# The fourth tile's queries and keys made in the first layer's time, and the second batch's means and keys taken in turns with the last values

## The chip, the cores and the metric

The kernel runs on one core of one Trainium2 chip. The time is device microseconds of one execution, and the figure that is compared is the median of several runs. A core has five engines that run side by side and wait for one another through semaphores: PE multiplies matrices, DVE and ACT do element-wise work and read the accumulators that PE writes, POOL does element-wise work in SBUF, and SP issues most of the transfers. Each engine takes its instructions strictly in the order in which they were written, so an instruction that waits holds up all that stand behind it on its engine.

## What is computed

```python
# q, k, v: [2, 8, 768, 64]
k_sum = k.reshape(B, H, 24, 32, D).max(axis=3)       # one key for each block of 32
v_sum = v.reshape(B, H, 24, 32, D).mean(axis=3)      # one value for each block of 32
scores_l = scale * q @ k.T                           # kept where |i - j| < 16, else -1e9
scores_s = scale * q @ k_sum.T + log(32)
a = softmax([scores_l, scores_s])
attn = a @ [v, v_sum]                                # -> x: [1536, 512]
h = x @ w_in                                         # layer one: [1536, 2048]
g = h * clip(h + 3, 0, 6) / 6
x2 = g @ w_out                                       # [1536, 512]
# then: 8 experts of 192 rows each, chosen greedily from the logits x2 @ w_gate,
# out[rows of e] = relu(x2[rows of e] @ w1[e]) @ w2[e]
```

All of it is in float32; a large product is taken as three products of a high and a low part.

## The kernel before, in words

The 1536 rows are cut into 12 tiles of 128 (numbered 0 to 11 in the code; six to a batch), and three tiles make a unit, so that units 0 and 1 are batch 0 and units 2 and 3 are batch 1. A tile `n` goes through attention in two halves of four heads, `(n, 0)` and `(n, 1)`:

- `q_prep(n)` transposes the tile's queries on PE (L343) and copies them with ACT (L345) into `qT`; `window(n)` copies the keys that the tile may see, and the block keys, into `kw` on DVE (L358 to L365).
- `front(n, h)` is the scores on PE (L377), mask and row maximum on DVE (L385, L387). Its argument `after` says whether it also makes the next tile's `q_prep` and `window`.
- `soften()` is the four exponentials on ACT (L397), the reciprocal on DVE (L399, L400) and the scaling on POOL (L401).
- `turn(n, h)` transposes the weights on PE (L409) and copies them with ACT (L414); `values(n, h)` multiplies them with the values on PE (L427). `emit_x()` then makes the tile's high part `xh` with ACT (L449) and its low part `xl` with DVE (L79, named after the line of the scheduler that issues deferred work).
- The values' tile `VW` holds the window's rows, loaded from DRAM, and below them the block means. `vsum_mean` makes the means of a batch on PE (L201), and `vsum_place` copies them into a `VW` with one ACT (L208) and one DVE instruction (L209). In the trace each of the two waits for the other: both read one accumulator.
- `kprep(b)` transposes the keys of batch `b` on PE (L325), copies them with ACT (L328), and takes the block maxima on DVE (L329).

The first layer is `gemm1(u)`: 16 slices `f` of 128 columns, each 12 matmuls (L620, L621, L622: high by high, high by low, low by high) into one accumulator, then a relu on ACT (L623) and the gate on DVE (L637). Its weights arrive as 64-bit words: `w_conv` makes float32 of them with three DVE instructions a slice (L275), `w_split` makes the high part on ACT (L292) and the low part on POOL (L293).

The order on each engine is the order in which the program writes the work, and `drive` sets it: it holds several generators ("streams"), each with a total cost and a span from `lo` to `hi`, and always takes the next step of the stream that is furthest behind, `lo + (hi - lo) * done / total`. Only the steps' yielded costs count, not times. First comes the prologue with the whole attention of unit 0 (`first_unit`). Then the first 8 slices of unit 0 are written in turns with the attention of tiles 3 to 5 and with the preparation of batch 1, then the first 8 slices of unit 1 with the start of tile 6, and so on, until attention is done within unit 2. The second product, the routing and the experts follow and do not take part in the change.

At the end of batch 0 `halves()` first drains what is left of tiles 4 and 5 (`drain`: a `turn`, its `values`, and `emit_x`, one after another), then makes three means, all keys and the other three means of batch 1. Then tile 6 begins: `vsum_place` twice, `q_prep(6)`, `window(6)`.

One point of the order matters more than it shows: `attend_unit(0)` ends when tile 2 is in `finished`, and this happens inside a step, so the step runs on to its next yield. Before, that takes in `front(3, 0)`.

Of the kernel before, what the change touches and what calls it, by code (L numbers as in the profile page):

```python
# [15 lines left out]
B, H, S, D = 2, 8, 768, 64  # L16
# [10 lines left out]
UT = 3  # L27
# [20 lines left out]
MEANS = {(1, 0): range(2), (1, 1): range(2, 4), (2, 0): range(4, 6)}  # L48
LOADS = {(3, 0): [("kraw", 0, j) for j in range(3)], (3, 1): [("kraw", 0, j) for j in range(3, 6)],
         (4, 0): [("vraw", 1, j) for j in range(3)], (4, 1): [("vraw", 1, j) for j in range(3, 5)]}  # L50
ATTS = [29066, 32816, 25780, 17002]
FILL = 6500, 8500
END = [0.92, 0.92, 0.92]
S0 = 0.78
# [35 lines left out]
def build(ctx, tc, q, k, v, w_in, w_out, w_gate, w1, w2, out):  # L90
# [30 lines left out]
    def bank(i):  # L121
        return psum.tile([128, 512], FT, name=f"bank{i}")
# [51 lines left out]
    def v_of(n):  # L174

        return VL if n == UT - 1 else VW[n % 2]
# [17 lines left out]
    def vsum_mean(b, js):  # L194

        for j in js:
            if j == 0:
                mp[b] = bank(5 if b == 0 else 4)
            x = raw.pop(("vraw", b, j))
            at = ZO - WIN - 4 * j  # L200
            PE.matmul(mp[b][:KEYS], zones[:, at:at + KEYS], x.rearrange("p h d -> p (h d)"),  # L201
                      start=j == 0, stop=j == S // 128 - 1)
            if b and j == 0:
                soon.append(partial(load_rows, "vraw", v, b, S // 128 - 1))
# [130 lines left out]
    def q_prep(n, hps=range(HP)):  # L335
        b, i = divmod(n, 6)
        x = raw["qraw", b, i]
        p = bank(6 if n == UT else (7 if n % 2 else 4) if n < UT else (4 if n % 2 else 7))
        a, z = hps[0], hps[-1] + 1
        if a == 0:  # L340
            fr[n] = att.tile([128, HP, 128], FT, name="qT"), att.tile([128, HP, 2, KEYS], FT, name="kw")
        for hp in hps:
            PE.transpose(p[:, hp * 128:(hp + 1) * 128],  # L343
                         x[:, 2 * hp:2 * hp + 2, :].rearrange("p h d -> p (h d)"), ident)
        ACT.activation(fr[n][0][:, a:z], p[:, a * 128:z * 128].rearrange("p (h s) -> p h s", s=128), AF.Copy)  # L345
        if n >= UT and (n + 1) % 6:
            soon.append(partial(load_rows, "qraw", q, *divmod(n + 1, 6)))
# [19 lines left out]
    def front(n, h, after):  # L367
        b, i = divmod(n, 6)
        qT, kw = fr[n]
        A = Abuf[(2 * n + h) % (LAG + 1)]  # L370
        sp = [bank(0), bank(1)]
        for pr in range(2):
            hp = 2 * h + pr
            for g in range(2):
                for s in range(2):
                    r, c = slice(64 * s, 64 * s + 64), slice(QG * g, QG * g + QG)
                    PE.matmul(sp[s][c, pr * KEYS:(pr + 1) * KEYS], qT[r, hp, c], kw[r, hp, g], start=True, stop=True)  # L377
        if after:
            q_prep(n + 1)
        mk = mask[:, 0 if i == 0 else 2 if i == 5 else 1]  # L380
        sm = att.tile([128, 4, 4], FT, name="sm", bufs=2)
        for pr in range(2):
            for s in range(2):
                c = 2 * pr + s
                DVE.tensor_tensor_reduce(out=A[:, c], in0=sp[s][:, pr * KEYS:(pr + 1) * KEYS], in1=mk, scale=1.0,  # L385
                                         scalar=-3e38, op0=OP.add, op1=OP.max, accum_out=sm[:, 0, c:c + 1])
        DVE.tensor_scalar(sm[:, 1], sm[:, 0], -SCALE, None, op0=OP.mult)  # L387
        if after:
            window(n + 1)
        later.append((A, sm))  # L390
# [78 lines left out]
    def first_unit():  # L469

        for n in range(UT):
            for h in range(2):
                if len(pend) >= LAG:
                    t = pend.pop(0)
                    turn(*t)
                    turned.append(t)
                    yield 660
                front(n, h, h == 1)
                pend.append((n, h))
                yield 1250 + 450 * h  # L480
                yield from soften()
                if (n, h) in MEANS:
                    vsum_mean(0, MEANS[n, h])
                    yield 900 * len(MEANS[n, h])
        for n in range(UT):
            vsum_place(0, v_of(n))
            t = pend.pop(0)
            turn(*t)
            turned.append(t)
            yield 660  # L490
            for h in range(2):
                values(*turned.pop(0))
                yield 1000
            yield from emit_x()

    def halves():
        yield from first_unit()
        for n in range(UT, NT):
            b, i = divmod(n, 6)
            if b and i == 0:  # L500
                for x in VW:
                    vsum_place(b, x)
                q_prep(n)
                window(n)
                yield 2400
            for h in range(2):
                t = pend.pop(0) if len(pend) >= LAG else None
                if t:
                    turn(*t)
                    turned.append(t)  # L510
                    yield 660
                after = h == 1 and i < 5
                front(n, h, after)
                pend.append((n, h))
                yield 1250 + 450 * after
                if len(turned) > 1:
                    values(*turned.pop(0))
                    yield 1000
                    yield from emit_x()
                yield from soften()  # L520
                if b + 1 < B:
                    for kind, src, j in LOADS.get((i, h), ()):
                        load_rows(kind, (k, v)[src], b + 1, j)
                if h == 1 and i == 4 and b + 1 < B:
                    load_rows("qraw", q, b + 1, 0)
            if i == 5:
                yield from drain()
                if b + 1 < B:
                    vsum_mean(b + 1, range(3))
                    yield 2700  # L530
                    yield from kprep(b + 1)
                    vsum_mean(b + 1, range(3, S // 128))
                    yield 2700
                    prepared.append(b + 1)

    turned, prepared = [], []
    attention = halves()
# [279 lines left out]
    for u, fs, att_stream, slices in ((0, half[0], [attend_batch(), ATTS[1]], 6),  # L817
                                      (1, half[0], [attend_for(FILL[0]), FILL[0]], 4),
                                      (0, half[1], [attend_for(FILL[1]), FILL[1]], 3),
                                      (1, half[1], [attend_unit(2), ATTS[2] - sum(FILL)], 0)):  # L820
        st = [att_stream + [0.01, 0.95]]
        if slices:
            n = 4 * slices + CLAG * (slices == 3)
            st.append([part(splitting, n), n, 0.0, 0.85 if slices > 3 else S1])
        drive([[gemm1(u, fs), G1 / 2, 0, 1]] + st, soon)
# [436 lines left out]
```

## Time and profile before

| | |
|---|---|
| median of 3 runs | 606.79 us (606.27 to 610.18) |
| the profiled execution | 610.91 us, of which the span from first to last instruction is 609.1 us |
| PE busy | 558.2 us (92% of the span) |
| DVE, ACT, POOL busy | 393.8, 292.3, 162.5 us |
| mean clock granted to TensorE | 0.97 of full speed |

The times of the rows below are microseconds from the start of the span of that execution. The prologue ends and the first layer's products begin at about 47 us; attention lasts until about 215 us. A granted clock of 0.50 is the lower of TensorE's two levels (1.2 GHz), 1.00 the upper (2.4 GHz).

### The profile page before, as it was taken

What the parts mean: (1) busy time and instruction counts of PE and PEld (TensorE: products, weight loads), DVE (VectorE), ACT (ScalarE), POOL (GpSimd) and SP (SyncE); (2) the same over time, 40 slices, a digit from 0 to 9 for tenths busy, and PEclk for the clock granted to TensorE, in tenths of its full rate; (3) what the DMA queues carried; (4) which work ended last, traced back from release to release, by engine and by line L of the source; (5) the groups of instructions that cost most, each with busy time, mean ns of one, the idle gap of its engine ahead of it and who ended that gap; (6) DMA issues with size and microseconds to landing.
All of it is one profiled execution on the core that took longest, in us unless ns stands there. A gap on an engine that the chain in (4) does not pass through costs nothing.

```text
span 609.1 us, 10859 instructions
## 1 busy us (share of the span) xinstructions
PE 558.2 (92%) x3791; PEld 466.4 (77%) x3791; DVE 393.8 (65%) x1204; ACT 292.3 (48%) x699; POOL 162.5 (27%) x194
## 2 busy tenths in 40 slices
PE   7766878899999998889999999999899999999994
PEld 6454756898889987775687777778688889988883
DVE  6546765874543279990007787873568888888880
ACT  4543734654545345451123232233466776776760
POOL 1312421433111024353245444446201001110111
PEclk9956999999999999999999999999899999999998
DMA  9958953311111055420015000003568889988811
GB/s 193 227 144 213 208 133 90 93 48 44 45 28 25 1 174 171 141 70 27 1 39 169 1 1 1 1 2 119 191 179 250 247 262 278 281 234 256 250 63 31
DMA packets 114432, 75.06 MB, mean 123 GB/s; under 512 B 59904, under 2 KB 100864, under 8 KB 114368
## 3 DMA queue, kind: packets, MB, share of 16 engines
q1 hardware_dynamic: 112384, 67.96, 41.6%
q0 software_dynamic: 1984, 6.32, 2.8%
q8 instruction: 32, 0.52, 0.4%
q14 instruction: 32, 0.26, 0.1%
HBM read 67.55 MB, written 6.71 MB: 122 GB/s over the span
## 4 chain that ended last, share of the span: by engine, by line
PE 49%; issue 26%; DVE 8%; POOL 5%; ACT 4%; SPq 4%; DMA 2%; POOLq 0%; DVEq 0%; ACTq 0%
PE bank L620 7%; PE bank L621 7%; PE bank L622 7%; PE bank L740 5%; PE bank L742 5%; PE bank L741 5%; POOL out_dram L1065 2%; PE bank L427 2%; PE bank L933 2%; POOL xs L671 2%; PE bank L649 2%; SPq L171 1%; PE bank L583 1%; PE bank L377 1%; ACT A L397 1%
## 5 line engine op out<-in xcount | busy, mean ns | idle before, releaser
L620 PE MATMUL bank<-x,wh 128*128 128x384 f32 x256 | 92.6, 362 | 1.0 <-DVE t L637 0.9
L302 DVE TENSOR_TENSOR wl<-t,wh 128x1024 fp32r<-128x1024 f32 x64 | 77.1, 1221 | 20.7 <-ACT wh L301 19.1
L717 ACT ACTIVATE work<-t 128x384 fp32r<-128x384 f32 (+2 forms) x80 | 36.3, 459 | 112.2 <-PE bank L741 106.6
L621 PE MATMUL bank<-x,wh 128*128 128x384 f32 x256 | 86.8, 339 | 2.7 <-DVE x L79 2.7
L622 PE MATMUL bank<-x,wl 128*128 128x384 f32 x256 | 87.2, 341 | 1.2 <-POOL wl L293 1.1
L718 POOL TENSOR_TENSOR tlx<-t,work 128x384 fp32r<-128x384 f32 (+1 forms) x58 | 60.6, 1045 | 81.4 <-ACT work L717 78.3
L740 PE MATMUL bank<-wh,work 128*128 128x512 f32 x192 | 78.7, 410 | 1.6 <-ACT work L717 0.8
L623 ACT ACTIVATE t<-bank,three 128x384 f32<-128x384 f32 x64 | 37.1, 580 | 82.4 <-PE bank L622 82.4
L742 PE MATMUL bank<-wh,tlx 128*128 128x512 f32 x192 | 75.8, 395 | 0.1
L741 PE MATMUL bank<-wl,work 128*128 128x512 f32 x192 | 75.6, 394 | 0.0
L1090 PE MATMUL bank<-x,wh 128*128 128x384 f32 x256 | 73.7, 360 | 0.5 <-DVE x L1016 0.5
L301 ACT ACTIVATE wh<-t 128x1024 fp32r<-128x1024 f32 x64 | 65.7, 1048 | 0.0
L637 DVE SCALAR_TENSOR_TENSOR t<-t,bank 128x384 f32<-128x384 f32 x64 | 35.0, 550 | 45.7 <-ACT t L623 45.5
L1092 PE MATMUL bank<-x,wl 128*128 128x192 f32 x256 | 64.2, 251 | 0.0
L1065 POOL DMA_INDIRECT out_dram<-t,idx x16 | 14.9, 934 | 141.6 <-DVE t L1114 136.0
L620 PEld LDWEIGHTS bank<-x,wh 128*128 128x128 f32 x256 | 48.9, 191 | 4.1 <-DVE t L637 1.5
L621 PEld LDWEIGHTS bank<-x,wh 128*128 128x128 f32 x256 | 48.9, 191 | 3.6 <-DVE x L79 3.4
L401 POOL TENSOR_TENSOR A<-A,sm 128x480 f32<-128x480 f32 x24 | 24.3, 1011 | 98.9 <-ACT at L414 47.0
L622 PEld LDWEIGHTS bank<-x,wl 128*128 128x128 f32 x256 | 48.6, 190 | 2.2 <-POOL wl L293 2.2
L1092 PEld LDWEIGHTS bank<-x,wl 128*128 128x128 f32 x256 | 48.9, 191 | 0.3
L1106 PE MATMUL bank<-wh,t 128*128 128x512 f32 x128 | 49.0, 392 | 0.0
L1090 PEld LDWEIGHTS bank<-x,wh 128*128 128x128 f32 x256 | 48.1, 188 | 1.2 <-DVE x L1016 0.8
(188 smaller groups left out, 1082.9 us busy)
## 6 DMA issues: line engine op xcount, KB each, us to landing
t<-in_moe_w_dram SPq DMA_DIRECT2D x128, 256.0 KB
t<-in_moe_w_in_dram SPq DMA_DIRECT2D x16, 512.0 KB
big<-in_moe_w_out_dram SPq DMA_DIRECT2D x16, 512.0 KB
VW<-in_v_dram SPq DMA_DIRECT2D x18, 192.0 KB
t<-in_v_dram SPq DMA_DIRECT2D x12, 256.0 KB
t<-xs SPq DMA_DIRECT2D x8, 258.0 KB
raw<-in_q_dram SPq DMA_DIRECT2D x8, 256.0 KB
t<-in_k_dram SPq DMA_DIRECT2D x12, 128.0 KB
```

The costliest lines, as they stand in the source:

```text
L301: ACT.activation(hi, x, AF.Copy)
L302: DVE.tensor_tensor(lo, x, hi.bitcast(FT), op=OP.subtract)
L620: PE.matmul(p, wh[:, kk, :], xh[:, kk, :], start=kk == 0, stop=False)
L621: PE.matmul(p, wh[:, kk, :], xl[:, kk, :], start=False, stop=False)
L622: PE.matmul(p, wl[:, kk, :], xh[:, kk, :], start=False, stop=kk == KD - 1)
L718: (DVE if placed[0] else POOL).tensor_tensor(ths[i][1], t, ths[i][0].bitcast(FT), op=OP.subtract)
L740: PE.matmul(acc[j], th[:, c], WH[s], start=f == 0, stop=False)
L741: PE.matmul(acc[j], th[:, c], WL[s], start=False, stop=False)
L742: PE.matmul(acc[j], tl[:, c], WH[s], start=False, stop=f == NF - 1)
L1090: PE.matmul(p, a[:, kk, :], xt[:, kk].rearrange("p c s -> p (c s)"), start=kk == 0, stop=False, skip_group_check=True)
L1092: PE.matmul(p[:, :CAP], b[:, kk, :], xt[:, kk, 0, :], start=False, stop=kk == KD - 1, skip_group_check=True)
L1106: PE.matmul(p, x, w, start=m == 0 and i == 0, stop=m == NM - 1 and i == 2)
```

## The change

Five edits, all on the order in which work is written:

1. `q_prep(3)` and `window(3)` no longer follow `front(2, 1)` in the prologue. They are written where tile 3 begins. Because of the point above, the step that ends `first_unit` now takes in these two instead of `front(3, 0)`, which moves behind the first slice of the first layer.
2. The means are placed into the values' tiles of tiles 0 and 1 right behind `front(2, 1)`; only tile 2's placing stays in the loop over tiles. Four products of the identity with itself (`warm(4)`, results unused) follow tile 0's values.
3. At the end of batch 0 a new generator `prepare(1)` (means by two, then keys, then means by two and two) is taken in turns with `drain()`, a step of each. The means of batch 1 get accumulator 0 instead of 4.
4. The attention streams next to the half units start at 0.04 instead of 0.01 of the products, and two totals in `ATTS` grow by what their streams now yield.
5. `q_prep` takes accumulator 4 for tile 3, where it was 6; for the other tiles the new expression gives the same as before.

```diff
--- before.py
+++ after.py
@@ -48,7 +48,7 @@
 MEANS = {(1, 0): range(2), (1, 1): range(2, 4), (2, 0): range(4, 6)}
 LOADS = {(3, 0): [("kraw", 0, j) for j in range(3)], (3, 1): [("kraw", 0, j) for j in range(3, 6)],
          (4, 0): [("vraw", 1, j) for j in range(3)], (4, 1): [("vraw", 1, j) for j in range(3, 5)]}
-ATTS = [29066, 32816, 25780, 17002]
+ATTS = [30216, 34066, 25780, 17002]
 FILL = 6500, 8500
 END = [0.92, 0.92, 0.92]
 S0 = 0.78
@@ -195,7 +195,7 @@
 
         for j in js:
             if j == 0:
-                mp[b] = bank(5 if b == 0 else 4)
+                mp[b] = bank(5 if b == 0 else 0)
             x = raw.pop(("vraw", b, j))
             at = ZO - WIN - 4 * j
             PE.matmul(mp[b][:KEYS], zones[:, at:at + KEYS], x.rearrange("p h d -> p (h d)"),
@@ -335,7 +335,7 @@
     def q_prep(n, hps=range(HP)):
         b, i = divmod(n, 6)
         x = raw["qraw", b, i]
-        p = bank(6 if n == UT else (7 if n % 2 else 4) if n < UT else (4 if n % 2 else 7))
+        p = bank((4, 7)[n % 2 == (n < UT)])
         a, z = hps[0], hps[-1] + 1
         if a == 0:
             fr[n] = att.tile([128, HP, 128], FT, name="qT"), att.tile([128, HP, 2, KEYS], FT, name="kw")
@@ -475,15 +475,19 @@
                     turn(*t)
                     turned.append(t)
                     yield 660
-                front(n, h, h == 1)
+                front(n, h, h == 1 and n < UT - 1)
                 pend.append((n, h))
                 yield 1250 + 450 * h
+                if (n, h) == (UT - 1, 1):
+                    for t in range(2):
+                        vsum_place(0, v_of(t))
                 yield from soften()
                 if (n, h) in MEANS:
                     vsum_mean(0, MEANS[n, h])
                     yield 900 * len(MEANS[n, h])
         for n in range(UT):
-            vsum_place(0, v_of(n))
+            if n == UT - 1:
+                vsum_place(0, v_of(n))
             t = pend.pop(0)
             turn(*t)
             turned.append(t)
@@ -492,6 +496,8 @@
                 values(*turned.pop(0))
                 yield 1000
             yield from emit_x()
+            if n == 0:
+                warm(4)
 
     def halves():
         yield from first_unit()
@@ -500,6 +506,7 @@
             if b and i == 0:
                 for x in VW:
                     vsum_place(b, x)
+            if n in (UT, 6):
                 q_prep(n)
                 window(n)
                 yield 2400
@@ -524,14 +531,25 @@
                 if h == 1 and i == 4 and b + 1 < B:
                     load_rows("qraw", q, b + 1, 0)
             if i == 5:
-                yield from drain()
+                both = [drain()] + ([prepare(b + 1)] if b + 1 < B else [])
+                while both:
+                    for x in list(both):
+                        c = next(x, None)
+                        if c is None:
+                            both.remove(x)
+                        else:
+                            yield c
                 if b + 1 < B:
-                    vsum_mean(b + 1, range(3))
-                    yield 2700
-                    yield from kprep(b + 1)
-                    vsum_mean(b + 1, range(3, S // 128))
-                    yield 2700
                     prepared.append(b + 1)
+
+    def prepare(b):
+
+        vsum_mean(b, range(2))
+        yield 1800
+        yield from kprep(b)
+        for j in range(2, S // 128, 2):
+            vsum_mean(b, range(j, j + 2))
+            yield 1800
 
     turned, prepared = [], []
     attention = halves()
@@ -818,7 +836,7 @@
                                       (1, half[0], [attend_for(FILL[0]), FILL[0]], 4),
                                       (0, half[1], [attend_for(FILL[1]), FILL[1]], 3),
                                       (1, half[1], [attend_unit(2), ATTS[2] - sum(FILL)], 0)):
-        st = [att_stream + [0.01, 0.95]]
+        st = [att_stream + [0.04, 0.95]]
         if slices:
             n = 4 * slices + CLAG * (slices == 3)
             st.append([part(splitting, n), n, 0.0, 0.85 if slices > 3 else S1])
```

Lines below L500 or so have moved by 18: L638, L639 and L640 of the new kernel are the matmuls L620, L621 and L622, L641 is the relu L623, and L655 is the gate L637.

Where the prologue ends, PE's order was this (L377 is `front`, L343 `q_prep(3)`, L409 a `turn`, L427 all values of tile 0, 1 and 2 in this order; accumulator 539 belongs to `front(3, 0)`):

```order
L377 MATMUL bank_403<-kw,qT 64x120
L343 MATMUL bank_412<-ident,t 128x128 x4
L409 MATMUL bank_441<-ident,A_92 120x128 x4
L427 MATMUL bank_447<-t,VW_93 64x64 x16
L409 MATMUL bank_469<-ident,A_89 120x128 x4
L427 MATMUL bank_479<-t,VW_94 64x64 x16
L409 MATMUL bank_505<-ident,A_90 120x128 x4
L427 MATMUL bank_513<-t 64x64 x16
L377 MATMUL bank_539<-kw,qT 64x120
```

Now it is this (L150 is `warm`, L638 and L639 the first two matmuls of the first layer):

```order
L377 MATMUL bank_403<-kw,qT 64x120
L409 MATMUL bank_429<-ident,A_92 120x128 x4
L427 MATMUL bank_435<-t,VW_93 64x64 x16
L150 MATMUL bank_455<-ident 128x128 x4
L409 MATMUL bank_460<-ident,A_89 120x128 x4
L427 MATMUL bank_468<-t,VW_94 64x64 x16
L409 MATMUL bank_494<-ident,A_90 120x128 x4
L427 MATMUL bank_503<-t 64x64 x16
L343 MATMUL bank_527<-ident,t 128x128 x4
L638 MATMUL bank_550<-x,wh 128x384
L639 MATMUL bank_550<-x,wh 128x384
```

The transposes of tile 3's queries went from the head of the last three turns to their end, and `front(3, 0)` left this place.

At the end of batch 0, ACT's order was this (accumulators 838, 887 and 931 are slices 3, 4 and 5 of unit 0; L414 are copies of turned weights, L449 makes `xh` of tiles 4 and 5, and L328, the first copy of keys, comes last):

```order
L623 ACTIVATE t<-bank_838,three 128x384
L292 ACTIVATE wh<-t 128x512
L414 ACTIVATE at<-bank_857 120x512
L449 ACTIVATE x<-bank_828 128x4x128
L414 ACTIVATE at<-bank_878 120x512
L623 ACTIVATE t<-bank_887,three 128x384
L292 ACTIVATE wh<-t 128x512
L414 ACTIVATE at<-bank_915 120x512
L623 ACTIVATE t<-bank_931,three 128x384
L449 ACTIVATE x<-bank_902 128x4x128
L292 ACTIVATE wh<-t 128x512
L328 ACTIVATE kT<-bank_962 128x4x128
```

Now it is this (accumulators 943, 985 and 1028 are slices 5, 6 and 7; 859 and 999 are the values of tiles 4 and 5):

```order
L328 ACTIVATE kT<-bank_932 128x4x128
L449 ACTIVATE x<-bank_859 128x4x128
L641 ACTIVATE t<-bank_943,three 128x384
L328 ACTIVATE kT<-bank_958 128x4x128
L414 ACTIVATE at<-bank_967 120x512
L292 ACTIVATE wh<-t 128x512
L641 ACTIVATE t<-bank_985,three 128x384
L292 ACTIVATE wh<-t 128x512
L414 ACTIVATE at<-bank_1012 120x512
L641 ACTIVATE t<-bank_1028,three 128x384
L449 ACTIVATE x<-bank_999 128x4x128
L208 ACTIVATE VW_93<-bank_848 24x512
```

Tile 5's `xh` went from behind slice 5, two slices ahead of the unit's end, to behind slice 7, the last of the half unit.

On DVE, tile 5's `xl` (L79, accumulator 902) stood ahead of the maxima of batch 1's keys (L329) and of the placing of its means (L209):

```order
L637 SCALAR_TENSOR_TENSOR t<-t,bank_931 128x384
L79 TENSOR_TENSOR x<-bank_902,x 128x4x128
L275 TENSOR_SCALAR t<-t 128x512
L329 TENSOR_REDUCE ks<-kT 128x4x4 x2
L275 SCALAR_TENSOR_TENSOR t<-t 128x512
L329 TENSOR_REDUCE ks<-kT 128x4x4
L637 SCALAR_TENSOR_TENSOR t<-t,bank_977 128x384
L329 TENSOR_REDUCE ks<-kT 128x4x4 x2
L275 SCALAR_TENSOR_TENSOR t<-t 128x512
L329 TENSOR_REDUCE ks<-kT 128x4x4
L209 COPY VW_93<-bank_950 24x512
L209 COPY VW_94<-bank_950 24x512
```

Now it (accumulator 999) stands behind the placing, behind tile 6's window (L358, L359, L365) and behind the gate of slice 7:

```order
L209 COPY VW_93<-bank_848 24x512
L209 COPY VW_94<-bank_848 24x512
L358 MEMSET kw 128x4x16
L359 COPY kw<-kT 128x4x80
L359 COPY kw<-kT 128x4x96
L365 COPY kw<-ks 128x4x24 x2
L655 SCALAR_TENSOR_TENSOR t<-t,bank_1028 128x384
L79 TENSOR_TENSOR x<-bank_999,x 128x4x128
L275 TENSOR_SCALAR t<-t 128x512
```

The next product on PE behind slice 7 and `q_prep(6)` is, in both kernels, the first slice of unit 1, whose second matmul reads the low parts of tiles 3, 4 and 5.

## Rows read from the trace of the kernel before

**Rows 1.** What PE waited for, 28.5 to 101 us: total us, times, longest us.

```profile
PE bank L343 <- DMA t<-in_q_dram: 4.1, 1, 4.1
PE bank L377 <- DVE kw L365: 3.8, 2, 3.4
PE bank L427 <- ACT at L414: 2.4, 3, 1.2
PE bank L201 <- DVE x L79: 1.9, 1, 1.9
PE bank L622 <- POOL wl L293: 1.1, 1, 1.1
```

**Rows 2.** Timeline of PE: start us, duration us, engine, line; idle before it in brackets.

```profile
32.70 0.82 PE L343 MATMUL bank<-ident,t 128*128 128x128 f32 x4 [4.14 <-DMA t<-in_q_dram]
...
50.54 0.69 PE L621 MATMUL bank<-x,wh 128*128 128x384 f32 x1 [2.43 <-DVE x L79]
...
54.02 0.64 PE L377 MATMUL bank<-kw,qT 64*64 64x120 f32 x16
...
58.66 1.09 PE L377 MATMUL bank<-kw,qT 64*64 64x120 f32 x16 [3.41 <-DVE kw L365]
```

**Rows 3.** Timeline of ACT and DVE around the prologue's end.

```profile
29.10 0.57 ACT L414 ACTIVATE t<-bank 120x512 f32<-120x512 f32 x1
...
30.48 0.31 DVE L387 TENSOR_SCALAR sm<-sm 128x4 f32<-128x4 f32 x1
...
34.11 0.39 ACT L397 ACTIVATE A<-A,sm 128x120 f32<-128x120 f32 x1
...
35.75 0.59 ACT L208 ACTIVATE VW<-bank 24x512 f32<-24x512 f32 x1
...
41.97 1.41 DVE L275 SCALAR_TENSOR_TENSOR t<-t 128x512 int32<-128x512 int32 x2
...
48.06 0.28 DVE L385 CUSTOM_DVE_ANT_0 A<-bank,mask 128x120 f32<-128x120 f32 x1
...
48.99 0.31 DVE L387 TENSOR_SCALAR sm<-sm 128x4 f32<-128x4 f32 x1
...
49.81 0.68 DVE L79 TENSOR_TENSOR x<-bank,x 128x512 fp32r<-128x512 f32 x1
```

**Rows 4.** Busy time by stretch: stretch, its us, each engine's busy us, PEclk, DMA.

```profile
36.40:47.40 11.00, 9.71 (x120) 7.71 (x120) 7.46 (x12) 5.51 (x10) 2.26 (x2) 0.50 0.47 119
57.00:60.00 3.00, 1.34 (x18) 1.06 (x19) 2.55 (x15) 1.62 (x8) 0.84 (x1) 0.50 0.96 215
```

**Rows 5.** Timeline behind the last matmul of slice 7, unit 0.

```profile
100.92 0.34 PE L622 MATMUL bank<-x,wl 128*128 128x384 f32 x1
...
101.29 0.58 ACT L623 ACTIVATE t<-bank,three 128x384 f32<-128x384 f32 x1 [3.87 <-PE bank L622]
...
101.45 0.42 PE L620 MATMUL bank<-x,wh 128*128 128x384 f32 x1
...
102.51 0.70 DVE L209 COPY VW<-bank 24x512 f32<-24x512 f32 x1 [3.87 <-ACT VW L208]
...
103.24 0.59 ACT L208 ACTIVATE VW<-bank 24x512 f32<-24x512 f32 x1 [0.76 <-DVE VW L209]
...
103.86 0.70 DVE L209 COPY VW<-bank 24x512 f32<-24x512 f32 x1 [0.66 <-ACT VW L208]
...
105.09 0.32 DVE L365 COPY kw<-ks 128x96 f32<-128x96 f32 x2
...
105.44 0.66 PE L377 MATMUL bank<-kw,qT 64*64 64x120 f32 x16 [1.66 <-DVE kw L365]
105.44 0.56 DVE L637 SCALAR_TENSOR_TENSOR t<-t,bank 128x384 f32<-128x384 f32 x1
```

**Rows 6.** What PE waited for, 101 to 215 us.

```profile
PE bank L377 <- DVE kw L365: 2.4, 2, 1.7
PE bank L620 <- DVE t L637: 0.9, 1, 0.9
```

## The prediction

> **What bounds the kernel now.** I read first what PE waited for between the prologue's last front and the end of the first half unit [rows 1], because nearly all of PE's idle time before 215 us lies there; from 101 us on PE waits for little [rows 6]. Then I followed the longest waits on the timelines. There are four. PE stands 4.14 us at `q_prep(3)`, until the fourth tile's queries land at 32.70 [rows 2]. ACT and DVE stand with it, since the exponentials of `(2, 1)` are queued behind the copy of those queries: they begin only at 34.11, and the first placing of means follows at 35.75 [rows 3]. At 50.54 the first layer's second matmul has waited 2.43 us for tile 2's low part, which DVE made at 49.81, behind `front(3, 0)`'s maxima and two slices of converted weights [rows 2, 3]. At 58.66 `front(4, 0)` has waited 3.41 us for its window [rows 2]. From 58.66 to 101.26, the end of slice 7 [rows 5], the waits for `at` (2.4), for tile 5's `xl` ahead of the first mean (1.9) and for a slice's low weights (1.1) make 5.4 us [rows 1]. PE is bound by other engines' queues throughout, so what counts is which instruction stands last in which queue. I make the sum on the profiled execution's span (609.1, its time 610.91) and take the difference off the median, 606.79.
>
> **Part A, up to the first layer's second matmul.** The wait for the transfer goes, since the transposes now come behind tile 2's values, long after 32.70. What is late next? ACT ends the copy of a turn at 29.67, DVE the maxima at 30.79 [rows 3]. The two placings then run in a chain, ACT 0.59 and DVE 0.70 each time [rows 3, 5]: the first ends at 31.5, the second at 32.8. ACT's four exponentials (34.11 to 35.75, so 1.64 [rows 3]) begin behind its second placing at 32.1 and end at 33.75. One copy of 0.6 later comes tile 0's `xh`, ready at 34.95. From here DVE is last: `xl` 0.69, three conversions (two are 1.41 [rows 3]; the third at 0.4 to 0.7, take 0.4) to 37.45, tile 2's placing 0.70 to 38.15, the second `xl` to 38.85, three conversions to 40.65, `window(3)` to 41.5 (0.85, as tile 6's from 104.56 to 105.41 [rows 5]), one conversion, then tile 2's `xl` at 42.6. PE's own chain is shorter: values of tile 2 from 38.2, under 2 us even at the lower clock, then `q_prep(3)` at 0.82 [rows 2]. So the second matmul starts at about 42.6 instead of 50.54, **8.0 earlier**. `warm(4)` is four more matmuls like those of L343, 0.4 to 0.8 us, beside DVE's chain: nothing, or 0.8 if PE were last. SP is not in the way: the loads that follow wait for PE's values and DVE's conversions, which also come earlier.
>
> **Part B, up to `front(4, 0)`.** `front(3, 0)` is now behind slice 0. Eleven matmuls of a slice took 3.48 at the lower clock (50.54 to 54.02 [rows 2]), so the slice ends at 46.1 and `front(3, 0)` at 47.1. Its maxima wait for the gate of slice 0 and a conversion ahead of them (0.58, 0.56, 0.7) and take 1.24 (48.06 to 49.30 [rows 3]), which puts `front(3, 1)` at 48.0. Then DVE has a conversion, the reciprocal behind the exponentials (48.7 to 50.3, then 0.4), the next maxima 1.2 and the window 0.9: `front(4, 0)` starts at about 52.8 instead of 58.66, with the same work done. **5.9 earlier** remains; 2.1 was given back because `front(3, 0)` no longer fills PE's wait for the low part.
>
> **Part C, up to the end of slice 7.** PE does the same work as before in another order. Of the 5.4 us of waits most go, since keys and means now stand between a turn and its values. New ones come, which no row shows as such. Slice 1 is now ahead of `front(5, 0)`: behind its end ACT has the relu 0.58 and the exponentials 1.64, DVE the reciprocal 0.4, maxima 1.24, window 0.9, 4.7 in all, against a front (0.64) and three sets of four transposes (0.5 each, an estimate from the 0.82 at the lower clock [rows 2]) on PE: a wait of 2.5. Slices 5 and 6 wait for their low weights, because ACT's high part now stands behind a copy of keys and a copy of a turn (0.6 each): about 1 each. The last values wait 0.9 for their turn's copy. Sum 5.4, as much as goes. The clock decides the rest. Before, PE ran at the lower level from 57 on [rows 4], until slice 1 had passed; now slice 1 follows `front(4, 0)` at once, and the level should rise again sooner. I take 1.0 of gain; the ends are -2 (two late weights cost 1.5 each and the 2.5 us wait drops the level again for two slices' fronts) and +3.5 (half the new waits are hidden). Slice 7 then ends 6.9 earlier, near 94.4.
>
> **Part D, the new wait.** Tile 5's `xh` is now queued on ACT behind slice 7's relu, its `xl` on DVE behind both placings, tile 6's window and slice 7's gate, and the next slice on PE, unit 1's first, needs it. Count from the end T of slice 7 (101.26 before). The relu ends at T+0.61 [rows 5], then `xh` 0.60, then the chain that ran from 101.89 to 105.41 before (placing on ACT, DVE, ACT, DVE, window: 3.52 [rows 5]) ends at T+4.75, the gate 0.56, `xl` 0.68: T+6.0. There unit 1's second matmul starts, with PE idle for about 4.5 us but for the transposes' end and one matmul. The slice takes 2.0 at the upper clock, 3.5 at the lower. Then `front(6, 0)` follows at once, at T+8.1 or T+9.6, its window long ready. Before it stood at T+4.18 (105.44), its wait of 1.66 included [rows 5]. So **3.9 or 5.4 are lost**; after 3.41 idle the level was 0.50 [rows 2, 4], so I take the lower clock, 5.4. A following slice and front at the lower level may cost up to 1.5 more, and the later waits for `kw` (0.7) and for a gate (0.9) [rows 6] would hide most of it: nil.
>
> Changes without a price: the mean's accumulator and the new `lo` and totals move a turn and a front by one slice in the part where PE hardly waits [rows 6].
>
> **Sum.** 8.0 - 2.1 + 1.0 - 5.4 = 1.5 us of gain: span 607.6, and 606.8 - 1.5 = **605.3**.
>
> **A rule weighed.** From 36.4 to 47.4 PE was busy 9.71 of 11.0 us, with values and turns, and the granted clock stayed at 0.50 [rows 4]; the first short front is the one behind slice 0, 0.64 at 54.02 [rows 2]. The Trainium skill's "TensorE: Matmul & The Clock Gate", Part 1, has it that the throttled state is the default and that activity releases it, and its section "Why this matters for your kernels" advises against idle gaps between bursts of matmuls. By that rule `warm(4)` and a shorter wait would keep the upper level through the prologue, and the time would be that of the first rival below, 601.8, instead of 605.3. The row disagrees for work of this shape; on the drop behind a gap they agree.
>
> **The rivals.**
>
> *The upper clock holds.* The wait ahead of tile 0's values falls from 4.14 us to two of about 1.2 with a few matmuls between. If that keeps the level, part A stays (DVE is last there), but slice 0, `front(3, 0)` and slice 1 are shorter by up to 3, of which DVE's round trips leave about 2, and part D costs 3.9: 8.0 - 2.1 + 1.0 + 2.0 - 3.9 = 5.0, so 601.8. For it: after waits of 1.89 and 1.66 matmuls were still short, 0.66 for a front [rows 5]. Against: the row of 36.4 to 47.4. The skill's rule above speaks for it. Chance 0.17.
>
> *The new wait does not bite.* If the parts of tile 5 were done while PE still has work of slice 7, parts A to C alone would count: 6.9 to 8, so 599.3. Against it: ACT and DVE take their queues in order, and the chain begins with slice 7's own relu. Chance 0.10.
>
> *Slower.* Low weights come late for slices 4 to 7, as ACT now has a copy of keys, a turn's copy and `xh` ahead of each high part. If each of the four waits 2 us instead of the two that I count at 1, part C is -5 instead of +1, and with the level down behind the new wait for two slices (1.5 more) the sum is 8.0 - 2.1 - 5 - 5.4 - 1.5 = -6: 612.8. It begins to lose where these waits pass 3.5 us together; with half of it 609. Against: PE too has keys, turns and values to do between the slices. Chance 0.13.
>
> *It does not do what it says*, for instance because the first values wait for something else than the placing: 607. Chance 0.05.
>
> **How the numbers follow.** The forecast has 0.55. Its own range is 603 to 608; to hold 8 in 10 it must take in the upper-clock case at 601.8 and the milder part of the slower one: 601.2 to 609.4. About 1% (6.1 us) is what a measurement of this kernel can tell from no change. Faster by more: the second rival and a third of the first, 0.16. Slower by more: a quarter of the slower one and some of what I do not see, 0.05. The same: 0.79.
>
> **What would show it.** No wait of PE for the queries' transfer, and exponentials of `(2, 1)` that start near 32. The first layer's second matmul near 42.6, `front(4, 0)` near 53, slice 7's end between 92 and 97. Then, as the step to look at first, one wait of 4 to 5 us of PE for DVE's `x` at the second matmul of unit 1's first slice, a granted clock of 0.50 behind it, and `front(6, 0)` 0 to 4 us ahead of 105.44. If that wait is missing, or short, or if late low weights add up to more than 3.5 us, I am wrong.

## The result and the profile after

The changed kernel takes 613.96 us (median of 20 runs, 610.83 to 616.09). The kernel before takes 610.46 (20 runs, 606.27 to 613.37; the three known ahead of the prediction, with a median of 606.79, are among them). The ratio is 1.0061, 95% interval 1.004 to 1.0081. Forecast were 1.5 us of gain, and a range that ended at 609.4: the kernel became slower by 3.5 us, and the time is outside the range. The forecast of 605.3 and 613.96 are 8.7 us apart. Of these, 3.7 come from the base, since the median of the three known runs lay that far below that of all twenty; the other 5.0 are the 1.5 of gain that did not come and the 3.5 of loss. The profiled execution took 611.98 us, its span 610.1; before it was 609.1.

PE's waits from 28.5 to 101 us, which answer to [rows 1]:

```profile
PE bank L639 <- DVE x L79: 5.9, 2, 4.3
PE bank L377 <- DVE kw L365: 5.7, 2, 3.4
PE bank L377 <- DVE sm L385: 2.0, 1, 2.0
PE bank L427 <- ACT at L414: 0.7, 1, 0.7
```

The wait for the queries' transfer is gone, and those for `at` fell from 2.4 to 0.7. The timeline of PE, to set beside [rows 2, 5]:

```profile
42.71 0.45 PE L639 MATMUL bank<-x,wh 128*128 128x384 f32 x1 [1.59 <-DVE x L79]
...
52.97 1.09 PE L377 MATMUL bank<-kw,qT 64*64 64x120 f32 x16 [3.38 <-DVE kw L365]
...
62.69 0.65 PE L377 MATMUL bank<-kw,qT 64*64 64x120 f32 x16 [2.35 <-DVE kw L365]
...
92.94 0.60 PE L343 MATMUL bank<-ident,raw 128*128 128x128 f32 x4
...
98.98 0.69 PE L639 MATMUL bank<-x,wh 128*128 128x384 f32 x1 [4.28 <-DVE x L79]
...
102.77 0.64 PE L377 MATMUL bank<-kw,qT 64*64 64x120 f32 x16
...
111.83 0.65 PE L377 MATMUL bank<-kw,qT 64*64 64x120 f32 x16 [0.76 <-DVE kw L365]
...
117.77 0.64 PE L377 MATMUL bank<-kw,qT 64*64 64x120 f32 x16
...
125.51 0.44 PE L638 MATMUL bank<-x,wh 128*128 128x384 f32 x1 [2.31 <-DVE t L655]
...
129.65 0.77 PE L377 MATMUL bank<-kw,qT 64*64 64x120 f32 x16
```

These are, in order: the first layer's second matmul, `front(4, 0)`, `front(5, 0)`, `q_prep(6)` behind slice 7, unit 1's second matmul, `front(6, 0)`, `(7, 0)`, `(7, 1)`, a slice that waits for a gate, and `front(8, 0)`. Down to `front(6, 0)` the trace goes as forecast in its main times; it is there 2.67 us ahead of 105.44 [rows 5]. The wait of 4.28 us has the chain that Part D describes: on ACT `xh`, then on DVE both placings, the gate of slice 7 and `xl`, the L79 that PE waits for:

```profile
93.62 0.59 ACT L449 ACTIVATE x<-bank 128x512 fp32r<-128x512 f32 x1
...
94.86 0.70 DVE L209 COPY VW<-bank 24x512 f32<-24x512 f32 x1 [4.95 <-ACT VW L208]
96.21 0.70 DVE L209 COPY VW<-bank 24x512 f32<-24x512 f32 x1 [0.66 <-ACT VW L208]
...
97.77 0.56 DVE L655 SCALAR_TENSOR_TENSOR t<-t,bank 128x384 f32<-128x384 f32 x1
98.24 0.68 DVE L79 TENSOR_TENSOR x<-bank,x 128x512 fp32r<-128x512 f32 x1
```

At `front(7, 1)` the lead is 3.15. Then comes what no step had: 2.31 us of waiting for a gate, and `front(8, 0)` stands 0.68 *behind*. The last values of attention start 0.63 behind as well. In the kernel before, the last turn ahead of `front(7, 1)` (L409), `front(7, 1)` and `front(8, 0)` were:

```profile
118.29 0.60 PE L409 MATMUL bank<-ident,A 128*120 128x128 f32 x4
...
120.92 0.64 PE L377 MATMUL bank<-kw,qT 64*64 64x120 f32 x16
...
128.97 0.64 PE L377 MATMUL bank<-kw,qT 64*64 64x120 f32 x16
```

DVE's timeline, with ACT's relu ahead of it, says why the gate is late. The slice's relu (ACT) began at 121.14, and its gate is the L655 at 124.92:

```profile
121.14 0.58 ACT L641 ACTIVATE t<-bank,three 128x384 f32<-128x384 f32 x1 [0.65 <-PE bank L640]
...
120.29 1.35 DVE L275 SCALAR_TENSOR_TENSOR t<-t 128x512 int32<-128x512 int32 x1
121.57 0.27 DVE L385 CUSTOM_DVE_ANT_0 A<-bank,mask 128x120 f32<-128x120 f32 x1
...
122.49 1.13 DVE L387 TENSOR_SCALAR sm<-sm 128x4 f32<-128x4 f32 x1
123.54 0.62 DVE L363 COPY kw<-kT 128x384 f32<-128x384 f32 x2
124.08 0.31 DVE L365 COPY kw<-ks 128x96 f32<-128x96 f32 x2
124.31 0.68 DVE L275 SCALAR_TENSOR_TENSOR t<-t 128x512 int32<-128x512 int32 x1
124.92 1.00 DVE L655 SCALAR_TENSOR_TENSOR t<-t,bank 128x384 f32<-128x384 f32 x2
```

The maxima of `(7, 1)`, its scaling (1.13 us; 0.17 in the kernel before), tile 8's window and a conversion now stand ahead of that gate. A slice's products go into one of two accumulators (`bank((5, 6)[f % 2])`), so PE stands until the gate has read the older one. Before, the front came a slice later than its turn, and a gate stood ahead of its maxima:

```profile
122.08 0.55 DVE L637 SCALAR_TENSOR_TENSOR t<-t,bank 128x384 f32<-128x384 f32 x1
...
123.26 0.27 DVE L385 CUSTOM_DVE_ANT_0 A<-bank,mask 128x120 f32<-128x120 f32 x1
...
124.18 0.17 DVE L387 TENSOR_SCALAR sm<-sm 128x4 f32<-128x4 f32 x1
```

Without that slice in between, DVE's work for the front and the gates of two slices fall together. About 1 us of the wait is the long scaling alone: it stands beside an instruction of POOL, and the last section returns to it. The busy times of the prologue's end, of the stretch up to `front(4, 0)` and beyond, and of the two new waits (columns as in [rows 4]):

```profile
36.40:47.40 11.00, 6.18 (x64) 5.00 (x64) 10.07 (x25) 3.41 (x6) 2.55 (x2) 0.84 0.79 195
49.00:58.00 9.00, 5.62 (x32) 4.84 (x31) 4.99 (x27) 3.24 (x14) 3.38 (x3) 0.50 1.26 239
...
93.00:102.80 9.80, 4.80 (x21) 3.91 (x19) 3.67 (x10) 2.84 (x5) 0.00 (x0) 0.65 0.33 67
...
126.00:129.00 3.00, 3.00 (x13) 2.90 (x12) 0.26 (x1) 0.10 (x1) 0.00 (x0) 0.59 0.00 0
```

Behind the wait for `xl` and behind that for the gate the granted clock falls: nine and six matmuls at 0.52 us where 0.34 is usual at the upper level.

### The profile page after: what moved, and what is told of

Read it like the earlier page. It is cut to its first block, busy times and chain, and to the rows that moved or that the text cites. A ratio compares the mean times of both kernels' runs of the same rounds, so it can differ in the third digit from the quotient of the medians.

```text
span 610.1 us, 10881 instructions
## 1 busy us (share of the span) xinstructions
PE 560.1 (92%) x3799; PEld 468.6 (77%) x3799; DVE 394.5 (65%) x1204; ACT 292.1 (48%) x699; POOL 162.5 (27%) x194
## 4 chain that ended last, share of the span: by engine, by line
PE 47%; issue 27%; DVE 10%; POOL 5%; ACT 5%; SPq 3%; DMA 2%; POOLq 0%; DVEq 0%; ACTq 0%
PE bank L638 7%; PE bank L640 7%; PE bank L639 7%; PE bank L758 5%; PE bank L760 5%; PE bank L759 5%; POOL out_dram L1083 2%; ACT A L397 2%; PE bank L951 2%; POOL xs L689 2%; PE bank L667 2%; PE bank L427 1%; PE bank L601 1%; SPq L171 1%; PE bank L377 1%
## 5 line engine op out<-in xcount | busy, mean ns | idle before, releaser
L638 PE MATMUL bank<-x,wh 128*128 128x384 f32 x256 | 93.5, 365 | 3.6 <-DVE t L655 2.7
L639 PE MATMUL bank<-x,wh 128*128 128x384 f32 x256 | 88.0, 344 | 6.2 <-DVE x L79 6.2
L640 PE MATMUL bank<-x,wl 128*128 128x384 f32 x256 | 88.5, 346 | 0.3 <-POOL wl L293 0.2
L735 ACT ACTIVATE work<-t 128x384 fp32r<-128x384 f32 (+2 forms) x80 | 36.4, 459 | 108.7 <-PE bank L759 105.7
L641 ACT ACTIVATE t<-bank,three 128x384 f32<-128x384 f32 x64 | 37.1, 579 | 91.2 <-PE bank L640 88.1
L1108 PE MATMUL bank<-x,wh 128*128 128x384 f32 x256 | 74.3, 361 | 0.0
L655 DVE SCALAR_TENSOR_TENSOR t<-t,bank 128x384 f32<-128x384 f32 x64 | 34.9, 549 | 51.8 <-ACT t L641 51.7
L639 PEld LDWEIGHTS bank<-x,wh 128*128 128x128 f32 x256 | 49.6, 194 | 7.3 <-DVE x L79 7.1
L638 PEld LDWEIGHTS bank<-x,wh 128*128 128x128 f32 x256 | 49.3, 193 | 7.0 <-DVE t L655 3.3
L640 PEld LDWEIGHTS bank<-x,wl 128*128 128x128 f32 x256 | 49.5, 193 | 1.5 <-POOL wl L293 1.3
```

The source lines that it names most:

```text
L638: PE.matmul(p, wh[:, kk, :], xh[:, kk, :], start=kk == 0, stop=False)
L639: PE.matmul(p, wh[:, kk, :], xl[:, kk, :], start=False, stop=False)
L640: PE.matmul(p, wl[:, kk, :], xh[:, kk, :], start=False, stop=kk == KD - 1)
L1108: PE.matmul(p, a[:, kk, :], xt[:, kk].rearrange("p c s -> p (c s)"), start=kk == 0, stop=False, skip_group_check=True)
```

## The experiments

The theory after this reading: two waits eat the gain, each a few us. One is tile 5's low part (forecast), one the gate that the streams' new 0.04 puts behind a front (not forecast). The rival: the loss lies elsewhere, above all in the clock's level or in `warm(4)`. Runs 1 to 4 shared a chip, 5 to 7 a second, 8 to 11 a third, each with the kernel before beside them.

**1. Tile 5's low part at once.** In the changed kernel's `emit_x`:

```
-            soon.append(partial(DVE.tensor_tensor, xl, px, xh.bitcast(FT), op=OP.subtract))
+            low = partial(DVE.tensor_tensor, xl, px, xh.bitcast(FT), op=OP.subtract)
+            low() if n == 5 else soon.append(low)
```

> The changed kernel, but tile 5's low part is written at once, ahead of the placing of the second batch's means, and not behind the next step. Theory (two new waits cost what the earlier part gains): PE's 4.28 us wait at the second matmul of unit 1's first slice falls under 1 us and the lower clock behind it goes; front(6, 0) then waits for its window and starts near 98.7 instead of 102.77; the time is 3 to 4 us under the changed kernel's, ratio to the kernel before about 1.000. Rival (DVE's and ACT's queues from 93 to 130 us set the end of that stretch, whatever PE waits for first): front(6, 0) is earlier, but what it gains is given back as a longer wait before 130 us, ratio 1.004 to 1.008 as now.

Measured: 607.56 against 610.22, ratio 0.994 [0.9903, 0.9976]. PE's timeline of this kernel at unit 1's second matmul, `front(6, 0)` and the gate's wait:

```profile
94.77 0.44 PE L639 MATMUL bank<-x,wh 128*128 128x384 f32 x1 [0.29 <-DVE x L450]
...
97.68 0.65 PE L377 MATMUL bank<-kw,qT 64*64 64x120 f32 x16 [0.73 <-DVE kw L365]
...
120.44 0.44 PE L638 MATMUL bank<-x,wh 128*128 128x384 f32 x1 [2.30 <-DVE t L655]
```

One instruction's place turns slower into faster. The ratio is lower than the theory's 1.000. The gate still waits 2.30, but here the clock stayed at 1.00 behind it:

```profile
120.00:126.00 6.00, 5.56 (x44) 4.99 (x44) 2.71 (x8) 2.57 (x10) 0.48 (x1) 1.00 0.00 0
```

**2. The later streams back at 0.01.** The first half unit keeps 0.04:

```
-        st = [att_stream + [0.04, 0.95]]
+        st = [att_stream + [0.04 if (u, fs[0]) == (0, 0) else 0.01, 0.95]]
```

> The changed kernel with the streams of the three later half units at 0.01 again (the first keeps 0.04), so that the first turn of tile 6 is written ahead of slice 5 of unit 1, as before the change. Theory of two waits: if the 2.31 us wait for a gate near 125 us comes from that order, it goes, and the time is 2 to 4 us under the changed kernel's, ratio about 1.000 to 1.003. Rival: DVE still reaches that gate near 125, PE waits for it there or just ahead of it, ratio 1.004 to 1.008.

Measured: 610.88 against 610.22, ratio 0.9974 [0.9938, 1.0009], which cannot be told from no change. This is the change with all that the prediction had priced, and without the new number of the later streams. The wait of 2.31 is gone (0.90 is left at a gate), the one for `xl` stays:

```profile
101.51 0.69 PE L639 MATMUL bank<-x,wh 128*128 128x384 f32 x1 [4.27 <-DVE x L79]
...
116.50 0.44 PE L638 MATMUL bank<-x,wh 128*128 128x384 f32 x1 [0.90 <-DVE t L655]
```

**3. Both.** Edits 1 and 2 together.

> Both edits together. Theory of two waits: 6 to 8 us under the changed kernel, ratio 0.993 to 0.997. Rival: ratio 1.003 to 1.008.

Measured: 607.13 against 610.22, ratio 0.9897 [0.9849, 0.9945]; the ratio rests on six runs here, and the two medians alone would make it 0.995, so it was repeated (10). All three ratios lie 0.3 to 0.6% below what the theory expected. That expectation had been worked out from the changed kernel's 1.0061, which run 8 below puts at 1.003.

**4. The prologue's part alone.** The changed kernel with the drain and the next batch's preparation one after the other as before, the means' accumulator in bank 4, and 0.01 for the later streams:

```
-                both = [drain()] + ([prepare(b + 1)] if b + 1 < B else [])
...
+                yield from drain()
```

> Only the prologue's part of the change: the fourth tile's queries and window in the first layer's time, the early placing, warm(4), 0.04 for the first half unit; the drain and the preparation stand one behind the other as before, the mean in accumulator 4, later streams at 0.01. Theory of two waits: front(4, 0) near 53 as in the changed kernel (58.66 before), no wait for tile 5's low part in unit 1, front(6, 0) 4 to 6 us ahead of 105.44; ratio 0.991 to 0.996. Rival: front(6, 0) is early, but by 130 us the lead is under 2 us, ratio 0.998 to 1.002.

Measured: 608.34 against 610.22, ratio 0.9964 [0.993, 0.9999], between theory and rival. `front(4, 0)` starts at 54.82 and `q_prep(6)` at 99.32, 1.8 earlier than before, and neither new wait shows. `front(6, 0)` is only 1.8 us ahead, not 4 to 6: of the 3.8 us won at `front(4, 0)`, 2.1 are lost again ahead of `q_prep(6)`, where `front(5, 0)` now waits 2.46 us for its window.

**5. The turns alone.** The kernel before with drain and preparation in turns, and bank 0.

> The kernel before with the third edit alone: drain and preparation in turns, means in accumulator 0. Theory of two waits: tile 5's low part lands behind placing, window and gate here too, so PE waits 4 to 4.5 us at the second matmul of unit 1's first slice and runs at the lower clock behind it; slice 7 ends 1 to 3 us earlier than 101.26, front(6, 0) stands 3 to 5 us later than 105.44; ratio 1.004 to 1.009. Rival (DVE's and ACT's queues set the end of the stretch): front(6, 0) is late but the time is the same, ratio 0.998 to 1.002.

Measured: 616.30 against 612.75, ratio 1.0058 [1.0028, 1.0088]. `front(6, 0)` is 2.3 us later than before (3 to 5 were expected). The wait is there in a kernel that has nothing else of the change:

```profile
103.91 0.69 PE L632 MATMUL bank<-x,wh 128*128 128x384 f32 x1 [4.27 <-DVE x L79]
...
107.73 1.08 PE L377 MATMUL bank<-kw,qT 64*64 64x120 f32 x16
```

**6. The later streams' number alone.** The kernel before with 0.04 for all but the first half unit:

```
-        st = [att_stream + [0.01, 0.95]]
+        st = [att_stream + [0.01 if (u, fs[0]) == (0, 0) else 0.04, 0.95]]
```

> The kernel before with the fourth edit's 0.04 for the three later half units alone; the first half unit keeps 0.01. Theory of two waits: the first turn of tile 6 is written behind slice 5 of unit 1, the exponentials of (7, 0) and the gate of slice 6 get late, PE waits about 2.3 us for that gate, and the clock drops in some runs: ratio 1.003 to 1.007. Rival (that wait comes from PE being early there, as the prologue's gain has it reach the gate ahead of DVE): no wait over 0.5 us, ratio 0.998 to 1.002.

Measured: 615.89 against 612.75, ratio 1.0048 [1.0019, 1.0076]. So 0.5% of loss comes from one number that the prediction had at nothing, and the trace shows the same wait as in the changed kernel:

```profile
130.93 0.44 PE L620 MATMUL bank<-x,wh 128*128 128x384 f32 x1 [2.31 <-DVE t L637]
```

**7. Without the warming matmuls.** The changed kernel without `if n == 0: warm(4)`.

> The changed kernel without the four products of the identity behind tile 0's values. Theory: they stand beside DVE's chain, and the clock of the stretch from 31 to 58 us does not hang on them: ratio as the changed kernel, 1.004 to 1.008. Rival (they keep the upper clock up in the prologue): slower by 1 to 3 us more, ratio 1.008 to 1.011.

Measured: 612.86 against 612.75, ratio 1.0003 [0.9984, 1.0022], below what either side expected. Since the changed kernel had been compared on another chip, the pair was run on one.

**8 to 11. Pairs on one chip:** the changed kernel again, the same without `warm(4)`, edits 1 and 2 together again, and these without `warm(4)`.

> The changed kernel once more, beside the same without its four warming matmuls, on one chip. Theory A, these matmuls cost what the first look without them gained (1.0003 against 1.0061): 1.004 to 1.008 here, and without them 0.998 to 1.002, so 0.4 to 0.8% apart. Theory B, the two comparisons differ because they ran on different chips, and the matmuls are free: both within 0.25% of each other, at 1.000 to 1.006. Waits as before: 4.3 us for tile 5's low part, 2.3 us for the gate near 125 us.

> The changed kernel without the four matmuls, on the chip of its pair. Theory A: 0.4 to 0.8% below the changed kernel. Theory B: within 0.25% of it. In the trace, by both: no wait near 40 us that the pair does not have, and the second matmul of the first layer within 0.5 us of the pair's.

> Tile 5's low part at once and 0.01 for the later streams, once more, since its first comparison rests on six runs: 0.985 to 0.9945 if that one was right; nearer 0.996 if it was luck. Against the changed kernel on the same chip 1.0 to 2.0% faster by both single effects taken together.

> The same without the four matmuls. Theory A: 0.4 to 0.8% faster than with them, so 0.980 to 0.990, and the best of all. Theory B: within 0.25% of it.

Measured against 611.70: 613.08 (1.003 [1.0003, 1.0056]) and without `warm(4)` 612.16 (1.0018 [0.9994, 1.0042]); 606.56 (0.9906 [0.9871, 0.994]) and 604.20 (0.9901 [0.9864, 0.9938]). With and without differ by 0.12% and 0.05% in the ratios; the medians are 0.9 and 2.4 us lower without, the second pair on nine and six runs. So theory A's 0.4 to 0.8% does not show, and that run 7's low ratio was a matter of the chip is the likelier reading; a small cost of these matmuls is not excluded. Both versions with edits 1 and 2 beat the kernel before by 0.9 to 1%, and the changed kernel by 6.5 us on the same chip (606.56 against 613.08).

**The stretches of all traces.** Worked out from the starts of `q_prep(6)`, `front(6, 0)`, `front(8, 0)` and the last values on PE:

| kernel | `q_prep(6)` at | to `front(6, 0)` | on to `front(8, 0)` | on to the last values |
|---|---|---|---|---|
| before | 101.09 | 4.35 | 23.53 | 82.53 |
| after | 92.94 | 9.83 | 26.88 | 82.48 |
| 1 (`xl` at once) | 92.73 | 4.95 | 25.50 | 82.35 |
| 2 (0.01) | 95.47 | 9.86 | 25.51 | 82.53 |
| 3, 10, 11 (both) | 95.89, 96.24, 94.76 | 4.95, 4.95, 4.96 | 25.00, 24.98, 23.53 | 82.54 to 82.55 |
| 4 (prologue) | 99.32 | 4.35 | 23.52 | 82.54 |
| 5 (turns) | 97.87 | 9.86 | 25.39 | 82.55 |
| 6 (0.04) | 102.55 | 4.35 | 28.04 | 82.62 |
| 7, 9 (no `warm`) | 94.05, 93.23 | 9.74, 9.86 | 26.90, 26.72 | 82.43, 82.68 |
| 8 (after again) | 95.17 | 9.86 | 26.80 | 82.77 |

The second column is 4.35 in the old turns, and in the new ones 4.95 or 9.7 to 9.9, by the place of tile 5's low part. The third is 23.5 to 25.5 with 0.01 and 25.5 to 28.0 with 0.04, on average 24.5 (seven traces) and 26.8 (six): 2.3 us. Where the clock stayed up it is 23.5 with 0.01 (before, 4, 11) and 25.5 with 0.04 (run 1), so the wait itself costs 2.0; where it fell behind the gate, 26.7 to 26.9 (after, 7, 8, 9). The 28.0 of run 6 has one more drop of the clock, 0.54 from 108 to 111 us, behind the 1.67 us wait at `front(6, 0)` that the kernel before has too (1.66, without the drop). The fourth is the same everywhere. Behind the last values the traces run on for 394.7 to 399.5 us, with no relation to the edits (394.7 in run 4, 399.5 in run 1): what the edits change lies in the first three columns.

## Why the prediction was wrong

*Part A, right.* 42.71 for 42.6, so 7.8 earlier for 8.0; no wait for the transfer, DVE's chain last, the exponentials from 31.94. Over the ten traces with this prologue it is 42.3 to 44.3.

*Part B, right in this trace by luck.* 52.97 for 52.8. But slice 0 ran at the upper clock, against the assumption, and `front(3, 0)` started at 44.84 instead of 46.1; from there to `front(4, 0)` it then took 8.13 instead of 6.7. In all ten traces with this prologue that stretch is 8.11 to 8.13, so Part B had it 1.4 too short. About 1.1 of it are the window's copies (L363), 1.69 us at 51.02 where the trace before has 0.61 at 57.78. In run 8, with the same instructions, slice 0 ran in part at the lower clock and `front(4, 0)` was at 54.65; over the ten traces it is at 53.0 to 56.2, 54.4 on average.

*Part C, right in its end, with a term too small.* The wait of `front(5, 0)` is 2.35 for 2.5, and slice 7 ends at 93.1 for 94.4; the late low weights that I counted at 1 each do not show among the waits (0.2 for `wl`). From `front(4, 0)` to `q_prep(6)` the nine traces with the turns take 39.7 to 41.4, before 42.4: 2.2 of gain on average for the 1.0 that I took. These 1.2 more and the 1.4 of Part B nearly cancel, so that slice 7 ends near 94.7 on average: the forecast time is right because two errors offset each other.

*Part D, right:* the wait is 4.28 for 4.5, the clock drops, and `q_prep(6)` to `front(6, 0)` is 5.48 longer, for 5.4. Runs 1 and 5 show the mechanism: the wait goes with one instruction's place, and comes with the turns alone. So at `front(6, 0)` the sum still held: 0.4 to 2.7 us ahead in the four traces with the whole change's order (after, 7, 8, 9), 1.8 on average, for 1.5.

*The step that failed* is the sentence "Changes without a price: the mean's accumulator and the new `lo` and totals move a turn and a front by one slice in the part where PE hardly waits [rows 6]". In the part where PE hardly waits, it then waited 2.31 us, and the lead of 2.67 at `front(6, 0)` was 0.68 of lag at `front(8, 0)`, 3.35 lost. Run 6 prices the new number by itself at 0.48%, 2.9 us (the interval is 1.2 to 4.7); the stretches give 2.0 for the wait and 3.2 to 3.4 with the lower clock behind it. Runs 1 and 3 differ by it too, 0.43% in the ratios, but their intervals overlap and their medians are 0.4 us apart, so they do not price it. I had taken the small waits of before as room. They were the result of an order in which a slice lay between a turn and a front. Moving the front by a slice put maxima, scaling and window (121.57 to 124.3) into the one gap of DVE in which the gate had to run. The price could have been bounded by rows of the trace before: 1.24 for maxima and 0.9 for a window were in Part B's own working, 2.1 together. The further 1 us of the scaling beside POOL is in none of them.

With 2.0 to 3.4 for it, the sum is 1.5 less that, 0.5 to 1.9 us slower, a ratio of 1.001 to 1.003; measured were 1.0061 and, in run 8, 1.003. What lies between the two measurements is not settled. Part D left up to 1.5 us for a lower clock behind the new wait at nil; runs 2 and 5, with that wait and 0.01, take 25.4 to 25.5 to `front(8, 0)`, but so nearly do runs 3 and 10 without it (25.0), so the clock's own variation is of that size.

*The rivals.* The new wait did bite. The upper clock did hold longer, 0.84 from 36.4 to 47.4 for 0.50 before [rows 4], with PE busy for less of that time; the wait ahead of that stretch had been 4.14 us [rows 2] and was now split into several under 1.4. The Trainium skill's "TensorE: Matmul & The Clock Gate", Part 1, has throttled as the default and activity as what releases it: the new order, with its shorter waits, fits that; the row of before, 0.50 with PE busy 9.71 of 11.0 us, still does not. But the time of that rival, 601.8, did not follow: from 49 to 58 the clock was 0.50 all the same, and `warm(4)`, to which I gave a share in it, is not needed for the higher level: without it that stretch had 0.84 in runs 9 and 11 and 0.69 in run 7, with it 0.81 to 0.90. The slower rival had the right sign by the wrong mechanism: late low weights cost 0.2 in all, not four times 2.

*The changed kernel's own merits:* the prologue's part alone gives 0.36%, and all of the change without its two waits 0.9 to 1%. By difference the turns, repaired, would be the larger part; that compares chips, and the intervals overlap, so it is not shown.

## What to carry to other kernels

When a change makes two producers take turns, follow every deferred instruction of the interrupted one (here a low part that is written a step later) to its new place in its queue, and look who reads it next: one line put back took that stretch from 9.83 to 4.95 us, 0.8% of the kernel. A stretch without waits is no reserve: before a step is called free there, write down the queue of the engine that feeds the bound one, with durations, as one would for a wait, and see what POOL does beside them. And price a retuned number alone, apart from the edits that came with it.

## What the runs showed of the hardware

The same waits can be followed by either clock. With 0.01, the slices behind the 0.90 us wait for a gate ran at 0.69 and 0.74 in run 10 (111 to 117 us) and at 1.00 in run 11 (same stretch), whose order differs only by `warm(4)`, some 75 us earlier; the two differ by 1.5 us to `front(8, 0)` through this alone. Run 10, then run 11:

```profile
111.00:114.00 3.00, 2.16 (x7) 2.16 (x8) 2.97 (x12) 0.65 (x4) 0.35 (x1) 0.69 0.13 22
114.00:117.00 3.00, 3.00 (x16) 2.93 (x16) 2.46 (x8) 1.21 (x3) 0.67 (x2) 0.74 0.47 156
...
111.00:114.00 3.00, 3.00 (x21) 2.96 (x20) 2.90 (x15) 1.21 (x3) 1.02 (x2) 1.00 0.53 162
114.00:117.00 3.00, 3.00 (x33) 2.60 (x32) 2.36 (x7) 2.81 (x11) 2.59 (x2) 1.00 0.42 117
```

Likewise the wait of 2.3 us was followed by the lower clock in five of the six traces that have it (0.59 in the changed kernel) and not in run 1 (1.00), while 4.3 us lowered it in all six traces with that wait. Between kernels with the same prologue, `front(4, 0)` starts anywhere from 52.97 to 56.24, and one trace cannot settle a us or two.

DVE's scaling of four maxima per row (L387) took 1.13 us at 122.49, beside the making of a low weight on POOL from 122.32 to 123.60, and 0.17 in the trace before, at 124.18, with POOL idle:

```profile
122.32 1.28 POOL L293 TENSOR_TENSOR wl<-t,wh 128x512 fp32r<-128x512 f32 x1 [1.22 <-ACT wh L292]
```

The pair is no accident. The thirteen traces have 312 of these scalings up to 230 us. All 121 that began with POOL idle took 0.17; all 191 that began while an instruction of POOL ran ended 0.01 to 0.06 us behind the end of that instruction, and took 0.17 to 1.24. At the late gate the scaling took 1.13 or 1.14 in all six traces with 0.04 and in none with 0.01. The window's copies of Part B, 1.69 instead of 0.61, end 0.2 behind an instruction of POOL in all ten traces. So these DVE instructions did not end before POOL's did; what the two share, no run shows.
